# The value products of an attention unit in one run instead of two

## Chip, core and metric

One core of a Trainium2 chip runs the whole kernel. The metric is the device time of one execution in microseconds. Below, PE is TensorE, DVE VectorE, ACT ScalarE, POOL GpSimd and SP SyncE, whose queue issues the DMAs.

## What is computed

Attention over 8 batches and 8 heads with 512 local and 32 global positions of 64 numbers, followed by a gated feed-forward layer over all 4,352 tokens. Local queries see the keys within 32 positions and the 32 global keys; global queries see all 544 keys.

```python
s_ll = np.where(mask, scale * q_l @ k_l.T, -1e9)       # |i - j| <= 32
a_l = sm(np.concatenate([scale * q_l @ k_g.T, s_ll], -1))
out_l = a_l @ np.concatenate([v_g, v_l], 2)
out_g = sm(scale * q_g @ k_all.T) @ v_all
x = concat(out_g, out_l) as (tokens, 512)
xn = x / rms(x) * rms_g
g, val = xn @ w_gate, xn @ w_val                       # 512 -> 1536 each
out = (silu(g) * val) @ w_out                          # 1536 -> 512
```

## The kernel before, in words

The tokens are worked on in nine chunks: eight batches of 512 local tokens and, last, the 256 global ones. While the feed-forward products of one chunk run on TensorE, the attention of a later chunk is done between them. The first two chunks follow an order that is written out by hand (`ORDER`); from chunk 2 on a small planner sets the order, and that is where the change lies.

A chunk's feed-forward work is a list of slots. In chunks 2 to 7 it has 42 slots of 12 fp16 products each (`moe_pair`, its products on line 1108, 7 slots for each of 6 groups) and then 24 slots of 6 products with w_out (`moe_block`, line 1266). After each slot's products the planner's `slot(1, c + 2)` (line 1406) walks through the attention steps that are still to be done and issues each one whose conditions hold, at most one of them with TensorE work. Then the slot's `rest` empties its product bank, on DVE or ACT. The wait for a step is counted in slots: `("A", ..., 1, [("T3", 2), ("V", 4)])` means step A, with TensorE work, at the earliest two slots after T3 and four after V.

The attention of a chunk from the third on consists of two local units (`local_halves`, lines 579 to 748), of four heads each, and one global unit. The steps of a local unit: L and V load queries, keys and values (SP); S makes the scores (line 665); M and N add the mask and find the extreme values on DVE (613), E and F take the exponentials on ACT (627), D divides (DVE 641, POOL 642), T transposes in blocks of 32 on DVE (647, into the tiles `et`); A and B multiply the transposed exponentials with the values (line 708); X and Y copy the result out of four PSUM banks, half by ACT (720) and half by DVE (721), square it (723) and sum the squares on POOL (725). There are twelve local units under the planner.

The values come in eleven key blocks. `blocks` (line 692) sets their order: block 10, the global keys, first, since it covers all queries and starts the sums; each further block adds to the queries that can see it. For each block there are four query/head parts and two heads, eight products on tiles of 32 rows by 64 columns of the array, in fp32. Each of these appears in the profile as two weight loads and two products, so that a unit has 88 products in the program and 176 PE rows and 176 PEld rows in the profile. Of these A has the first five blocks (80 rows) and B the other six (96 rows): `SPLIT, BGAP = 5, 2` (line 93). B comes two slots after A, X one slot after B, Y two after X. The next unit's V waits for B (`"^B"`) in the planner, since it loads into the same tiles.

Of the kernel before, what the change touches and what calls it, by code (L numbers as in the profile page):

```python
# [20 lines left out]
B, H, SL, SG, D = 8, 8, 512, 32, 64  # L21
# [46 lines left out]
def attention_moe_kernel(  # L68
# [21 lines left out]
    EARLY = 2  # L90
    SECOND = 64
    LG = (4, 8)
    SPLIT, BGAP = 5, 2
    GG = (6, 5, 4, 3)
    NORM = {1: (20, 19, 17, 16)}
    NORMS = (22, 21, 19, 17)
# [136 lines left out]
    def attn_bank(name):  # L233
        return psum.tile([P, 512], F32, tag="pa", bufs=4, name=name)
# [192 lines left out]
    def x_part(c, hp):  # L427

        ch = chunks[c]
        if hp % 2 == 0:  # L430
            ch["xx", hp // 2] = pool.tile([P, 2, 512], F32, tag="x", bufs=2, name=f"x{c}_{hp}")
        return ch["xx", hp // 2][:, hp % 2, :]
# [146 lines left out]
    def local_halves(c, b, hp, xt):  # L579
        u = b * (H // 4) + hp  # L580
        w = u - EARLY * (H // 4)
        st = {}
# [93 lines left out]
        def queries(et, m):  # L676

            if m == 10:
                x = et.rearrange("p (b x) -> p b x", b=2)[:, :, 64:448]
                return 0, 8, x.rearrange("p b (t x) -> p b t x", x=96)[:, :, :, QT : 2 * QT]  # L680
            lo, hi = max(0, m - 2), min(7, m)
            n = hi - lo + 1
            a, g = divmod(lo, 4)
            j = m - 4 * a
            o = a * 544 + g * P + (j + (j >= 3) - g) * QT
            if n == 1:
                return lo, n, et[:, o : o + QT]
            off = 0 if o + n * 96 <= 1088 else 64
            x = et[:, o - off : o - off + n * 96].rearrange("p (t x) -> p t x", x=96)
            return lo, n, x[:, :, off : off + QT]  # L690

        blocks = (10, 2, 3, 4, 5, 6, 7, 1, 8, 0, 9)

        def values(ms):
            if ms[0] == blocks[0]:
                st["a"] = [attn_bank(f"a{u}{p}") for p in range(4)]
            ps = st["a"]
            for m in ms:
                for p in range(4):
                    r = slice(p * QT, (p + 1) * QT)  # L700
                    for x in range(2):
                        lo, n, e = queries(st["et"][x][r], m)
                        o = ps[p][x * D : (x + 1) * D, lo * QT : (lo + n) * QT]
                        if n == 8:
                            o = o.rearrange("p (b t q) -> p b t q", b=2, q=QT)
                        elif n > 1:
                            o = o.rearrange("p (t q) -> p t q", q=QT)
                        nc.tensor.matmul(  # L708
                            o,
                            st["v"][x][r, m * D : (m + 1) * D],  # L710
                            e,
                            start=(m == blocks[0]),
                            stop=(m == blocks[-1]),
                            skip_group_check=True,
                        )

        def take(z):
            x = x_part(c, 2 * hp + z)
            xt.append(x)
            nc.scalar.copy(x[:, :256], st["a"][2 * z][:, :256])  # L720
            nc.vector.tensor_copy(x[:, 256:], st["a"][2 * z + 1][:, :256])
            sq = pool.tile([P, 512], F32, tag="w", bufs=3, name=f"sq{u}{z}")
            nc.scalar.activation(sq, x, AF.Square)
            if len(xt) > 1:
                nc.gpsimd.tensor_tensor(sq, sq, chunks[c]["sq"], ALU.add)
            chunks[c]["sq"] = sq

        steps = [
            ("L", load, 0, [("^S", 0)]),
            ("V", load_v, 0, [("^B", 0)]),  # L730
            ("S", scores, 1, [("L", LG[1]), ("^Y", 1)]),
        ]
        wide = 2 if c == EARLY else 3
        for j, (x, bk) in enumerate(((0, 0), (1, 0), (0, 1), (1, 1))):
# [6 lines left out]
                (f"T{j}", lambda x=x, bk=bk: turn(x, bk), 0, [(f"D{j}", 2)]),  # L741
            ]
        return steps + [
            ("A", lambda: values(blocks[:SPLIT]), 1, [("T3", 2), ("V", 4)]),
            ("B", lambda: values(blocks[SPLIT:]), 1, [("A", BGAP)]),
            ("X", lambda: take(0), 0, [("B", 1)]),
            ("Y", lambda: take(1), 0, [("X", 2)]),
        ]

# [612 lines left out]
    for c in range(NCH):  # L1362
        units = [(c, hp, "local") for hp in range(H // 4)] if EARLY <= c < B else []
        for i, g in enumerate(gplan[c]):
            units.insert(i + 1, (g,))
        for i, un in enumerate(units):
            if len(un) == 3:
                xi, steps = 2 * un[1], local_halves(c, c, un[1], chunks[c]["x"])
            else:
                xi, steps = -1, global_unit(*un)  # L1370
            kind = len(un)
            named = {}
            for name, fn, pe, after in steps:
                st = {"name": name, "fn": fn, "pe": pe, "c": c, "x": xi, "after": [], "at": None}
                st["from"] = (FIRST if c == EARLY else UNIT[len(units)])[i]
                for dep, gap in after:
                    if dep[0] == "^":
                        d = seen.get((kind, dep[1:]), [None])[-1]
                    else:
                        d = named[dep]  # L1380
                    if d is not None:
                        st["after"].append((d, gap))
                named[name] = st
                todo.append(st)
                chunks[c]["left"] += 1
            for name, st in named.items():
                seen.setdefault((kind, name), []).append(st)
# [249 lines left out]
```

## Time and profile before

| | |
|---|---|
| median of 3 runs | 935.0 us |
| lowest and highest run | 931.99 and 935.5 us |
| span of the profiled execution, first to last instruction | 930.2 us |
| mean granted TensorE clock | 0.989 |

The time of the profiled execution itself, with what lies around its span, is not listed; the span is 1.8 us under the lowest run and 4.8 under the median. In a profile row, "x" is the number of instructions, and what stands in brackets is the idle time just before, with the engine and operation that ended it; "issue" there means that nothing in the profile explains the idle time. A row of the waits gives the total, the number of times and the longest. A row of the windows gives, for a stretch of time, each engine's busy time and its number of instructions. PE rows are products, PEld rows are weight loads. The chain is the chain of waits that ended last.

### The profile page before, as it was taken

To read this page: it belongs to the slowest core of one execution; us is meant where nothing else is said; L and a number is where in the kernel's file an instruction comes from. 1 tells how busy PE (TensorE), PEld (TensorE's weight loads), DVE (VectorE), ACT (ScalarE), POOL (GpSimd) and SP (SyncE) were. 2 spreads that over 40 slices of the span, in tenths; PEclk is the share of its full clock that TensorE was granted. 3 is DMA by queue.
4 is the path that set the end of the run, shared out by engine and by line. 5 is a ranking of instruction groups with operands and counts; after the bars stand their busy time and mean duration, and the time that the engine had idled before them with its cause. 6 is when DMAs were issued, how large, how long until landed. Compare 5 with 4: busy or idle time off the path is not lost.

```text
span 930.2 us, 26398 instructions
## 1 busy us (share of the span) xinstructions
PE 893.9 (96%) x11028; PEld 612.2 (66%) x11028; DVE 634.0 (68%) x1603; ACT 495.4 (53%) x1232; POOL 253.8 (27%) x219
## 2 busy tenths in 40 slices
PE   5489999999999999999999999999999999999998
PEld 4444455545447885688648874788568865886584
DVE  6999987887884588557775679357846774664331
ACT  6999994555443564456344655356445732543131
POOL 0000000142423262334332353236233432332020
PEclk9699999999999999999999999999999999999999
DMA  9972533686449854495609771685349632787000
GB/s 352 407 288 96 159 120 115 209 265 198 144 119 320 282 180 147 133 299 169 213 24 279 242 238 43 200 279 184 139 136 297 190 95 79 248 273 238 35 1 23
DMA packets 83495, 173.40 MB, mean 186 GB/s; under 512 B 6705, under 2 KB 25393, under 8 KB 83377
## 3 DMA queue, kind: packets, MB, share of 16 engines
q1 hardware_dynamic: 82944, 171.40, 56.1%
q8 instruction: 86, 1.41, 0.6%
q10 hardware_dynamic: 432, 0.33, 0.1%
q14 instruction: 33, 0.26, 0.1%
HBM read 150.21 MB, written 21.50 MB: 185 GB/s over the span
## 4 chain that ended last, share of the span: by engine, by line
PE 82%; DVE 8%; DMA 4%; ACT 3%; issue 1%; POOL 1%; ACTq 0%; DVEq 0%; POOLq 0%
PE pq L1108 36%; PE po L1266 23%; PE p L1205 9%; PE a L708 4%; PE po L1333 3%; PE s L665 3%; DMA k<-in_qk_dram 2%; DMA v<-in_vw_dram 1%; DMA wr<-in_w_in_dram 1%; PE ga L838 1%; PE gs L781 1%; PE gt L824 1%; DVE wf L373 1%; ACT wr L272 1%; DVE t L1302 1%
## 5 line engine op out<-in xcount | busy, mean ns | idle before, releaser
L1108 PEld LDWEIGHTS <-wt 128*128 128x128 f16 x3024 | 292.6, 98 | 40.9 <-issue 5.3
L1266 PE MATMUL po<-wo,h 128*128 128x512 f16 x1080 | 236.2, 379 | 0.0
L1108 PE MATMUL pq<-xh,wt 128*128 128x256 f16 x1152 | 204.3, 273 | 0.0
L1266 PEld LDWEIGHTS <-h 128*128 128x128 f16 x1080 | 105.2, 98 | 123.9 <-issue 1.0
L1108 PE MATMUL pq<-xl,wt 128*128 128x256 f16 x576 | 157.0, 273 | 0.0
L1108 PE MATMUL pq<-ht,wt 128*128 128x256 f16 x1296 | 155.6, 273 | 0.9 <-issue 0.9
L642 POOL TENSOR_TENSOR e<-e,sm 128x512 f32<-128x512 f32 x48 | 50.0, 1042 | 291.4 <-DVE sm L641 287.6
L158 POOL TENSOR_TENSOR h<-t,h 128x512 f16<-128x512 f32 (+1 forms) x90 | 102.4, 1145 | 95.1 <-ACT h L1248 54.2
L1205 PE MATMUL p<-xh,wf 128*128 128x512 f16 x384 | 119.4, 382 | 6.9 <-DVE t L1302 6.3
L1205 PEld LDWEIGHTS <-wf 128*128 128x128 f16 x576 | 55.9, 99 | 74.4 <-issue 12.4
L1140 POOL TENSOR_TENSOR s<-s,s 128x512 f32<-128x512 f32 x36 | 48.2, 1339 | 190.6 <-ACT s L1137 117.9
L627 ACT ACTIVATE e<-e,sm 128x128 f32<-128x128 f32 x192 | 75.2, 393 | 36.6 <-DVE sm L613 36.5
L1170 ACT CAST h<-t 128x512 f16<-128x512 f32 x72 | 44.4, 616 | 57.3 <-DVE t L1162 56.7
L1205 PE MATMUL p<-xl,wf 128*128 128x512 f16 x192 | 73.5, 383 | 0.0
L1162 DVE SCALAR_TENSOR_TENSOR t<-t,c_h,v 128x512 f32<-128x512 f32 x72 | 70.7, 989 | 0.0
L1151 ACT ACTIVATE t<-u,half_inv 128x512 f32<-128x512 f32 x72 | 48.1, 715 | 38.7 <-DVE u L1126 28.6
L1126 DVE TENSOR_TENSOR v<-pq,s 128x512 f32<-128x512 f32 x72 | 49.6, 689 | 24.5 <-PE pq L1108 23.8
L1139 DVE TENSOR_TENSOR s<-pq,s 128x512 f32<-128x512 f32 x36 | 24.9, 691 | 44.3 <-PE pq L1108 42.2
L1133 ACT COPY s<-pq 128x512 f32<-128x512 f32 x36 | 21.0, 584 | 51.3 <-PE pq L1108 51.3
L613 DVE CUSTOM_DVE_ANT_0 e<-s,maskb 128x128 f32<-128x128 f32 x192 | 45.8, 278 | 2.8 <-PE s L665 2.8
L1126 DVE TENSOR_TENSOR u<-pq,s 128x512 f32<-128x512 f32 x36 | 24.9, 691 | 32.9 <-PE pq L1108 24.5
L1158 DVE SCALAR_TENSOR_TENSOR t<-t,u 128x512 f32<-128x512 f32 x72 | 46.9, 679 | 0.5 <-ACT t L1151 0.5
(352 smaller groups left out, 1281.5 us busy)
## 6 DMA issues: line engine op xcount, KB each, us to landing
wt<-wd SPq DMA_DIRECT2D x120, 512.0 KB, 4.8
wr<-in_w_in_dram SPq DMA_DIRECT2D x24, 512.0 KB, 9.9
k<-in_qkb_dram SPq DMA_DIRECT2D x24, 448.0 KB, 6.6
gkq<-in_gkq_dram SPq DMA_DIRECT2D x16, 576.0 KB, 6.5
wt<-wd SPq DMA_DIRECT2D x36, 256.0 KB, 4.7
out_dram<-o SPq DMA_DIRECT2D x34, 256.0 KB, 2.1
v<-in_vb_dram SPq DMA_DIRECT2D x24, 352.0 KB, 7.1
v<-in_vw_dram SPq DMA_DIRECT2D x16, 512.0 KB, 9.7
```

Source lines behind the costliest of these rows:

```text
L158: nc.gpsimd.tensor_tensor(dst, a, b, ALU.subtract)
L613: nc.vector.tensor_tensor_reduce(out=e[:, g, :], in0=ps[:, g * P : (g + 1) * P], in1=late["mask"][:, m * P : (m + 1) * P], scale=-0.125, s ...
L627: nc.scalar.activation(e[:, g, :], e[:, g, :], AF.Exp, bias=sm[:, 0, j + g : j + g + 1], scale=-1.0, accum_out=sm[:, 1, j + g : j + g + 1],)
L642: nc.gpsimd.tensor_tensor(e, e, r.unsqueeze(2).to_broadcast([P, 4, P]), ALU.mult)
L1108: nc.tensor.matmul(ps[:, j * HT : (j + 1) * HT], w[:, j, i, k * P : (k + 1) * P], x[:, k * HT : (k + 1) * HT], start=first, stop=(p in end ...
L1126: nc.vector.tensor_tensor(o, ps, x.rearrange("p (j n) -> p j n", j=2), ALU.add)
L1140: nc.gpsimd.tensor_tensor(s(6), s(6), s(1), ALU.add)
L1151: nc.scalar.activation(t, st["u"][:, j, :], AF.Tanh, scale=half_inv[:, f : f + 1])
L1158: nc.vector.scalar_tensor_tensor(t, t, 1.0, u, ALU.add, ALU.mult)
L1162: nc.vector.scalar_tensor_tensor(t, t, c_h[:, f : f + 1], st["v"][:, j, :], ALU.mult, ALU.mult)
L1205: nc.tensor.matmul(ps[:, :n], rows[:, a, o : o + P], ch[z][k][:, :n], start=(k == 0 and i == 0), stop=(k == NK - 1 and i == 2),)
L1266: nc.tensor.matmul(ps[0], ch["h", f][:, a, j * P : (j + 1) * P], wo[f][:, z, :], start=(f == 0 and q == 0), stop=(f == NF - 1 and q == 2),)
```

## The change

From the third chunk on, the unit's values are one step, A, over all eleven blocks. B is gone, with `SPLIT` and `BGAP`. X now comes one slot after A, and the next unit's V waits for A.

```diff
-    SPLIT, BGAP = 5, 2
...
-        def values(ms):
-            if ms[0] == blocks[0]:
-                st["a"] = [attn_bank(f"a{u}{p}") for p in range(4)]
-            ps = st["a"]
-            for m in ms:
+        def values():
+            ps = st["a"] = [attn_bank(f"a{u}{p}") for p in range(4)]
+            for m in blocks:
...
-            ("V", load_v, 0, [("^B", 0)]),
+            ("V", load_v, 0, [("^A", 0)]),
...
-            ("A", lambda: values(blocks[:SPLIT]), 1, [("T3", 2), ("V", 4)]),
-            ("B", lambda: values(blocks[SPLIT:]), 1, [("A", BGAP)]),
-            ("X", lambda: take(0), 0, [("B", 1)]),
+            ("A", values, 1, [("T3", 2), ("V", 4)]),
+            ("X", lambda: take(0), 0, [("A", 1)]),
             ("Y", lambda: take(1), 0, [("X", 2)]),
```

On TensorE, this is the place in the fourth unit (343.88 us in the profile) where A's first five blocks end. `a` are the four result banks, `et` the transposed exponentials, `v` the values, `pq` a product bank of the feed-forward layer, `wt` its weights. Before:

```order
L708 MATMUL a_4643<-et_4288,v_4020 64x96
L708 MATMUL a_4643<-et_4289,v_4022 64x96
L1108 LDWEIGHTS wt_51_4384
L1108 MATMUL pq_5_4591<-ht_3553,wt_51_4384 128x256
...
L1108 MATMUL pq_5_4608<-xh_3570,wt_52_4422 128x256
L708 MATMUL a_4640<-et_4288,v_4020 64x96
L708 MATMUL a_4640<-et_4289,v_4022 64x96
```

The same place with the change (line 705 is line 708 of before, 1104 is 1108):

```order
L705 MATMUL a_4643<-et_4288,v_4020 64x96
L705 MATMUL a_4643<-et_4289,v_4022 64x96
L705 MATMUL a_4640<-et_4288,v_4020 64x96
L705 MATMUL a_4640<-et_4289,v_4022 64x96
...
L705 MATMUL a_4643<-et_4289,v_4022 64x32
L1104 LDWEIGHTS wt_51_4384
L1104 MATMUL pq_5_4591<-ht_3553,wt_51_4384 128x256
```

The two slots of 12 feed-forward products that stood between the two parts now stand behind the second. Nothing else moves on TensorE: the scores and the global unit's steps keep their places.

On DVE, this is the place behind the fifth unit's run (385.35 us), where a chunk begins. `x` is the attention result, copied from the banks `a`; the additions with `s`, `v` and `u` empty product banks. Before:

```order
L1279 TENSOR_SCALAR o_5215<-po_5127,kk 128x512
L721 COPY x_0_5311<-a_5172 128x256
L1139 TENSOR_TENSOR s_0_5294<-pq_0_5298,s_0_5294 128x512
L1126 TENSOR_TENSOR v_5336<-pq_0_5218,s_0_5294 128x2x256
L721 COPY x_0_5311<-a_5174 128x256
L1126 TENSOR_TENSOR u_5357<-pq_0_5298,s_0_5231 128x2x256
```

With the change (718 is 721 of before, 1275 is 1279, 1135 is 1139, 1122 is 1126):

```order
L1275 TENSOR_SCALAR o_5263<-po_5127,kk 128x512
L718 COPY x_0_5279<-a_5172 128x256
L718 COPY x_0_5279<-a_5174 128x256
L1135 TENSOR_TENSOR s_0_5299<-pq_0_5303,s_0_5299 128x512
L1122 TENSOR_TENSOR v_5341<-pq_0_5266,s_0_5299 128x2x256
L1122 TENSOR_TENSOR u_5357<-pq_0_5303,s_0_5284 128x2x256
```

Both copies now stand ahead of the additions. ACT's copies and squares and POOL's sums (lines 720, 723 and 725) move by the same two slots; the order of SP's DMAs is the same, word for word.

## Prediction

> **What bounds the kernel now.** I read the page first, then the stretches of the steady chunks, then who makes TensorE (PE) wait, and last the rows around one pair of value runs.
>
> ```profile
> span 930.2 us, 26398 instructions
> PE 893.9 (96%) x11028; PEld 612.2 (66%) x11028; DVE 634.0 (68%) x1603; ACT 495.4 (53%) x1232; POOL 253.8 (27%) x219
> q8 instruction: 86, 1.41, 0.6%
> 445.00:545.00 100.00, 100.00 (x1382) 74.23 (x1380) 67.08 (x172) 51.19 (x141) 37.31 (x32) 1.00 0.59 189
> ```
>
> In a steady chunk of 100 us TensorE is never idle, and the next engine, DVE, works for two thirds of it. So a microsecond added to or taken from TensorE's stream there reaches the end, and work moved on DVE, ACT, POOL or SP does not unless it makes TensorE wait. After 190 us it waits for this, and no more:
>
> ```profile
> PE a L708 <- DVE et L647: 2.5, 2, 2.1
> PE pq L1108 <- issue: 0.9, 1, 0.9
> PE a L708 <- issue: 0.2, 1, 0.2
> ```
>
> The first row is the wait of two value runs for the last transposed exponentials (at 242 and 284 us). The other two are waits for nothing that the profile names, and they turn out to price this change.
>
> **The change on TensorE: the seam.** Here is one pair of runs, at 343.88 and 348.08 us, with the products around it.
>
> ```profile
> 343.57 0.27 PE L1108 MATMUL pq<-xl,wt 128*128 128x256 f16 x1
> 343.68 0.27 PE L1108 MATMUL pq<-xh,wt 128*128 128x256 f16 x1
> 343.88 1.54 PE L708 MATMUL a<-et,v 32*64 32x256 f32 x80
> 345.35 1.48 PE L1108 MATMUL pq<-ht,wt 128*128 128x256 f16 x12
> ...
> 347.87 0.27 PE L1108 MATMUL pq<-xh,wt 128*128 128x256 f16 x1
> 348.08 1.31 PE L708 MATMUL a<-et,v 32*64 32x96 f32 x96
> 349.32 0.28 PE L1108 MATMUL pq<-xh,wt 128*128 128x256 f16 x1
> ```
>
> Products start 0.11 us apart; going into a value run costs 0.20 and coming out again some 0.15 after the last value product's start. The second run costs TensorE 349.32 - 347.87 - 0.11 = 1.34 us. Its 96 products themselves, from the first start to the last, take 1.31 less the last one's own 0.22, so 1.09. Joined to the first run it pays no entry and no exit of its own: at most 1.34 - 1.09 = 0.25 us saved. [...] Nothing is computed less: the 176 products of a unit stay.
>
> **The change on the other engines.** The copies of step X (ACT 0.37 us, DVE 0.42), its square and POOL's sum come two slots earlier, Y's too, and SP may load the next values two slots earlier.
>
> ```profile
>   DVE x L721: 33.4, 11
>   ACT x L720: 8.8, 11
> SPq L602 <- PE a L708: 9.2, 3, 8.3
> ```
>
> These are waits of other engines for the value products: DVE stands 33.4 us in all at the head of its queue for them. Behind DVE's copy stand the additions that empty the product banks (L1139, L1126), but those need products that TensorE makes only after the run, so a copy of 0.42 us ahead of them is hidden in the next slot of 1.3 us. If that cover went, it would cost 24 times 0.42, 10 us; with a third of DVE idle I cost it at nothing. SP's order stays word for word. Its loads only come free sooner, and TensorE waits for no load after 190 us. The two waits for the transposes stay as they are: the run starts in its old slot, and the transposes are not moved.
>
> **The change on instruction supply.** This is the term that decides. The queue q8 brings 86 packets for 22,056 TensorE instructions (11,028 products and as many weight loads): 256 each. Where TensorE stopped for no named reason:
>
> ```profile
> 421.58 0.83 PE L1108 MATMUL pq<-ht,wt 128*128 128x256 f16 x6
> 423.33 0.83 PE L1108 MATMUL pq<-ht,wt 128*128 128x256 f16 x6 [0.92 <-issue]
> ...
> 289.06 0.80 PE L708 MATMUL a<-et,v 32*64 32x96 f32 x45
> 290.07 0.77 PE L708 MATMUL a<-et,v 32*64 32x64 f32 x51 [0.21 <-issue]
> ...
> 390.55 0.03 issue
> 390.57 0.45 PE a L708 x27
> ```
>
> The stops end at 423.33, 290.07 and 390.57. I counted the instructions between these ends:
>
> ```profile
> 290.06:423.32 133.26, 132.31 (x1916) 102.17 (x1915) 86.58 (x215) 66.56 (x169) 46.99 (x39) 1.00 0.66 215
> 390.56:423.32 32.76, 31.83 (x511) 27.46 (x511) 19.53 (x43) 15.13 (x29) 9.46 (x8) 1.00 0.88 289
> ```
>
> 3,831 lie between the first two, nine short of 15 times 256, and 1,022 between the last two, two short of 4 times 256; the few missing are waits that stand in TensorE's queue as instructions of their own. So all three stops fall exactly on the border between two packets. The packet before each, found by narrowing the window of the DMA view until it just held one, ran from 420.70 to 421.82, from 287.70 to 288.62 and from 388.11 to 389.07, in this order:
>
> ```profile
> q8 instruction: 1, 0.02, 6.0%
> ...
> q8 instruction: 1, 0.02, 6.0%
> ...
> q8 instruction: 1, 0.02, 6.0%
> ```
>
> TensorE went on 1.51, 1.45 and 1.50 us after the packet's end. I read this as starvation: a packet's instructions can be used 1.5 us after it lands, and it is asked for about when TensorE enters the page before. A stretch that burns 256 instructions faster than that makes TensorE wait. Products burn 24 in 1.31 us, 14 us a page. A value run burns 160 in the 1.30 us between the first and last start of its first part, and 192 in the 1.09 of its second: under 2 us a page. Neither part alone holds a page; joined they hold 352.
>
> [...]
>
> Where the page borders lie in each unit follows by counting from the border at 290.07 to the unit's first product:
>
> ```profile
> 290.06:343.87 53.81, 53.80 (x734) 47.24 (x733) 35.44 (x91) 32.09 (x83) 21.47 (x19) 1.00 0.78 250
> 290.06:385.35 95.28, 95.28 (x1232) 70.28 (x1231) 66.30 (x171) 50.25 (x138) 37.28 (x31) 1.00 0.58 191
> 290.06:445.15 155.09, 154.13 (x2115) 121.58 (x2114) 102.50 (x263) 83.51 (x223) 58.99 (x50) 1.00 0.64 209
> 283.53:290.06 6.53, 5.92 (x151) 4.42 (x150) 1.34 (x2) 1.17 (x2) 0.78 (x2) 1.00 0.99 318
> ```
>
> At 343.88: 1,467, so the next border (1,536) is 69 instructions into the unit, 67 with the waits counted. At 385.35: 2,463 against 2,560, about 91 with six waits. At 445.16: 4,229 against 4,352, about 113 with ten. At 283.9, counted backwards: 301 less 256, about 44. From 343.88 to 445.16 the border moves 46 later, and it does so with each further chunk: 138, 160, 185, 207, 232, 254 in the later units. Only where the first border falls before about 130 does the second one, 256 on, fall in the joined run of 352 or just behind it. Those are four units: 283.9, 343.9, 385.35 and 445.16. Two more packets, from 345.55 to 346.74 and from 447.45 to 448.76, serve the second and the fourth:
>
> ```profile
> q8 instruction: 1, 0.02, 6.1%
> ...
> q8 instruction: 1, 0.02, 6.1%
> ```
>
> The unit at 343.88, step by step: it passes the first border at 344.5, as before. The second, at instruction 323, it would reach at 345.2 + 163 x 5.7 ns = 346.1. The packet can be used at 346.74 + 1.5 = 348.2: a stop of 2.1 us. Then 29 instructions (0.2 us), the exit (0.15) and the two slots of products that used to stand between the runs (24 at 0.109, 2.6 us): the next product starts at 351.2 against 349.32 before, **+1.9 us**. Before, those two slots covered the wait; now they come after it.
>
> The other three take their ends from the chain:
>
> ```profile
> 290.84 0.22 PE pq L1108
> ...
> 391.02 0.22 PE pq L1108
> ...
> 450.66 0.21 PE pq L1108
> ```
>
> At 283.9: usable at 290.1 in both; before, 100 instructions were left and the slots done (290.8), now 52 are left and then 2.6 us of products, 293.2: **+2.4**. At 385.35: usable at 390.57; 391.0 before, 393.4 now: **+2.4**. At 445.16: the border lies 17 instructions behind the run, reached at 448.7, usable at 448.76 + 1.5 = 450.26; then 31 instructions of products, 1.7 us, and the pipeline: 452.1 against 450.66, **+1.4**.
>
> **The sum.** Stops 2.4 + 1.9 + 2.4 + 1.4 = +8.1; the seam in the eight other units 8 x -0.2 = -1.6. Together +6.5 us, 0.7%, on the profiled span of 930.2. The runs' median of 935.0 lies 4.8 above that span, the lowest, 931.99, only 1.8; I add the shift to the median: **941.5**.
>
> Bounds: from the first border to use it took 5.0, 3.7, 4.4 and 4.2 us in the four units. If every packet were as quick as 3.7, +4.5 would be left. If slow, a unit loses at most its two slots, about 2.5, and a fifth unit (486.6, border 42 instructions behind the run) up to 0.9: +8.5. With the runs' own scatter of 3.5 us, from 938 to 944.5 for this case.
>
> **Rivals.** *The fetch is hidden*: the stops were of another kind, or the packet is asked for sooner when the run burns faster. For it: the stops of before add up to under 2 us in 700. Then the seam alone counts: 932.6, not slower. It decides where packets can be used within 1.8 us of the first border; the quickest here took 3.7. [...] Chance 0.16. *The earlier copies and loads shorten DVE's busy stretch* from 192 to 245 us, so that the wait of 2.1 us for the transposes goes as well and fetch stays hidden: 935.0 - 2.4 - 2.5 = 930.1. Against it: only two copies pass the fold's sums there, and DVE's work is the same. Chance 0.05. *More units starve*: the value loads now start under the packet of a run and hold it up, so that the units at 545, 587 and 746 us stop too, at 1.5 us each: 946. Against it: their second border lies 60 or more instructions behind the run, or the packet lands before the run begins. Chance 0.07. The forecast keeps 0.72.
>
> **Chances.** Half a per cent, 4.7 us, is about what a measurement of this kernel can tell from no change. Of the forecast's 0.72, 0.56 lies above 939.7 and 0.16 below; with the third rival slower has 0.62. The first rival and the rest of the forecast make the same, 0.32; faster has 0.06, the second rival and the first one's scatter. The range 933 to 944.5 holds nearly all of the forecast and about half of the first rival.
>
> **What would show it.** Right: in the four units the joined run reads as two groups with an idle of 2 to 3 us on TensorE put down to issue, ending 1.5 us after a q8 packet, and the joined runs of the other units read as one group of some 2.4 us (the two first ones aside, where the transposes may be waited for). Wrong: all twelve runs of one piece and a span near 928; or idle put down to et, to a load, or to a bank that a copy holds.

## The result, and the profile after

| | before | after |
|---|---|---|
| median of 6 runs | 934.7 us | 944.17 us |
| lowest and highest | 931.99 and 936.04 us | 941.98 and 948.48 us |
| the profiled run | 931.99 us, span 930.2, clock 0.989 | 948.48 us, span 946.7, clock 0.978 |

The change makes the kernel 1.0% slower: ratio 1.0102, 95% interval 1.0084 to 1.0121, or 9.5 us between the medians. The profiled run of before is the quickest of its six and that of after the slowest of its six, so the two traces lie 16.5 us apart, more than the kernels do; the rows below explain the 16.5, and a later section says what of it is left in the medians.

First the page of after: the span, the busy times, the packets of q8, and the shares of the chain.

```profile
span 946.7 us, 26404 instructions
PE 900.2 (95%) x11028; PEld 618.2 (65%) x11028; DVE 624.1 (66%) x1603; ACT 495.3 (52%) x1232; POOL 252.7 (27%) x219
q8 instruction: 86, 1.41, 0.6%
PE 82%; DVE 9%; DMA 4%; ACT 3%; issue 2%; POOL 0%; ACTq 0%; DVEq 0%
```

TensorE has the same 11,028 products and is still the bound, but two things have grown: its busy time, by 6.3 us for the same work, and "issue" in the chain. The waits of TensorE after 190 us give the second its size:

```profile
PE a L705 <- issue: 7.1, 3, 2.9
PE pq L1104 <- issue: 4.1, 3, 1.9
PE a L705 <- DVE et L646: 2.5, 2, 2.1
```

The wait for the transposes is what it was. The unnamed waits went from 1.1 us to 11.2. Here they are on TensorE's timeline, in the third to the sixth unit; the number in brackets is the idle time ahead of the row:

```profile
286.76 1.25 PE L705 MATMUL a<-et,v 32*64 32x96 f32 x88
290.93 0.66 PE L705 MATMUL a<-et,v 32*64 32x32 f32 x27 [2.91 <-issue]
...
350.00 2.38 PE L705 MATMUL a<-et,v 32*64 32x256 f32 x160
354.52 0.35 PE L705 MATMUL a<-et,v 32*64 32x32 f32 x16 [2.15 <-issue]
...
395.12 2.55 PE L705 MATMUL a<-et,v 32*64 32x256 f32 x172
399.74 0.42 PE L705 MATMUL a<-et,v 32*64 32x32 f32 x4 [2.07 <-issue]
...
461.70 1.05 PE L1104 MATMUL pq<-ht,wt 128*128 128x256 f16 x8
464.64 1.04 PE L1104 MATMUL pq<-ht,wt 128*128 128x256 f16 x4 [1.90 <-issue]
...
503.98 2.58 PE L705 MATMUL a<-et,v 32*64 32x256 f32 x176
```

Three value runs are broken near their ends (16 products of 176 are left in the second, 4 in the third); the fourth run is whole and the stop lies eight products behind it. The last row is a unit with nothing missing, one group of 2.58 us. The packet of q8 ahead of each stop, found by narrowing the DMA view:

```profile
q8 instruction: 1, 0.02, 3.0%
...
q8 instruction: 1, 0.02, 3.4%
...
q8 instruction: 1, 0.02, 5.1%
...
q8 instruction: 1, 0.02, 4.9%
```

They ended at 289.70, 353.12, 398.30 and 463.36; TensorE went on 1.23, 1.40, 1.44 and 1.28 us later. Two more stops of the kind stand outside the value runs: 1.80 us at 437.26 behind the products of a step S, which was 0.92 us at 423.33 in before, and 0.44 us at 543.40.

Now the busy time. These are rows of after's chain: what stands behind the four stops, and the same stretches behind two units without one.

```profile
285.75 2.26 PE a L705 x103
288.01 2.91 issue
291.59 14.65 PE pq L1104 x108
350.07 2.31 PE a L705 x117
352.38 2.15 issue
354.87 7.01 PE pq L1104 x48
...
400.16 13.30 PE pq L1104 x108
...
464.64 6.10 PE pq L1104 x40
...
504.05 2.51 PE a L705 x129
506.56 11.90 PE pq L1104 x108
562.89 2.51 PE a L705 x133
565.40 5.35 PE pq L1104 x48
```

The same 108 products took 11.90 us in one place and 14.65 and 13.30 behind a stop; 48 took 5.35 and 7.01; and 40, which at that pace would take 4.41, took 6.10. They were slower because the granted clock was halved there, 0.50 against 1.00. The windows show where (us, TensorE's busy time and its instructions, the granted clock, DMA share, GB/s):

```profile
351.81:355.22 3.41, 1.26 (x76) 1.00 0.66 206
355.22:358.63 3.41, 3.41 (x18) 0.50 0.93 293
396.18:399.59 3.41, 1.49 (x131) 1.00 0.82 217
433.72:437.13 3.41, 1.74 (x82) 1.00 0.51 163
437.13:440.55 3.42, 3.29 (x31) 1.00 0.51 160
```

Behind the stop at 354.52 the clock is 0.50 for one stretch of 3.41 us. The stop at 437.26 leaves the clock alone. In all there are five such drops after 190 us, from 246.0 (behind the wait for the transposes), 290.37, 355.22, 399.59 and 464.45; the one from 290.37 lasts 6.83 us, the others 3.41. Before had none between 190 us and the end.

### The profile page after: what moved, and what is told of

It is laid out like the page before. It is cut to its first block, busy times and chain, and to the rows that moved or that the text cites. A ratio compares the mean times of both kernels' runs of the same rounds, so it can differ in the third digit from the quotient of the medians.

```text
span 946.7 us, 26404 instructions
## 1 busy us (share of the span) xinstructions
PE 900.2 (95%) x11028; PEld 618.2 (65%) x11028; DVE 624.1 (66%) x1603; ACT 495.3 (52%) x1232; POOL 252.7 (27%) x219
## 3 DMA queue, kind: packets, MB, share of 16 engines
q8 instruction: 86, 1.41, 0.6%
## 4 chain that ended last, share of the span: by engine, by line
PE 82%; DVE 9%; DMA 4%; ACT 3%; issue 2%; POOL 0%; ACTq 0%; DVEq 0%
PE pq L1104 36%; PE po L1262 22%; PE p L1201 9%; PE a L705 3%; PE po L1329 3%; PE s L664 3%; DMA k<-in_qk_dram 2%; DMA v<-in_vw_dram 1%; DMA wr<-in_w_in_dram 1%; PE ga L834 1%; PE gs L777 1%; PE gt L820 1%; ACT wr L271 1%; DVE t L1301 1%; DVE t L1298 1%
## 5 line engine op out<-in xcount | busy, mean ns | idle before, releaser
L1104 PEld LDWEIGHTS <-wt 128*128 128x128 f16 x3024 | 297.2, 99 | 47.1 <-issue 8.4
L1104 PE MATMUL pq<-xh,wt 128*128 128x256 f16 x1152 | 206.4, 276 | 0.4 <-issue 0.4
L1104 PE MATMUL pq<-ht,wt 128*128 128x256 f16 x1296 | 159.6, 277 | 3.7 <-issue 3.7
L1158 DVE SCALAR_TENSOR_TENSOR t<-t,c_h,v 128x512 f32<-128x512 f32 x72 | 61.1, 855 | 0.0
L722 POOL TENSOR_TENSOR sq<-sq,sq 128x512 f32<-128x512 f32 x18 | 23.0, 1276 | 92.1 <-ACT sq L720 76.0
```

The costliest lines, as they stand in the source:

```text
L1104: nc.tensor.matmul(ps[:, j * HT : (j + 1) * HT], w[:, j, i, k * P : (k + 1) * P], x[:, k * HT : (k + 1) * HT], start=first, stop=(p in end ...
L1158: nc.vector.scalar_tensor_tensor(t, t, c_h[:, f : f + 1], st["v"][:, j, :], ALU.mult, ALU.mult)
```

## The experiments

All ratios are to the kernel before on the same chip.

**The joined run alone.** X and V are put back to their old places, so that DVE, ACT, POOL and SP do everything in before's order.

```diff
-            ("V", load_v, 0, [("^A", 0)]),
+            ("V", load_v, 0, [("^A", 2)]),
...
-            ("X", lambda: take(0), 0, [("A", 1)]),
+            ("X", lambda: take(0), 0, [("A", 3)]),
```

> The values in one run, but X, Y and the next unit's value load two slots later, so that DVE, ACT, POOL and SP have the very order of before: only TensorE's stream is changed. Starvation (TensorE comes to a page border before the packet can be used): as slow as the change, 941 to 946 us, with the same four stops in the third to sixth unit. Moved steps (the earlier copies and loads do the harm): back at 932 to 935 us, with no stops in the runs.

945.16 us, ratio 1.0114 (1.0089 to 1.0139): all of the loss is still there. So are the waits:

```profile
PE a L705 <- issue: 7.3, 3, 3.7
PE pq L1104 <- issue: 3.2, 3, 1.9
```

The four stops end at 292.26, 354.80, 399.15 and 460.43, in the same units. Two smaller ones are in the second row: 0.58 us at 505.31, in the products behind the seventh unit's run, and 0.73 at 540.43. The earlier copies and loads neither cost nor brought anything that shows.

**The borders moved by half a packet.** The changed kernel with 64 tiny products more in an early group, 128 instructions for TensorE, so that every later border falls 128 instructions elsewhere. If the borders decide, other units stop. The control is the kernel before with the same products.

```diff
-            for j, f in enumerate(fs):
+            for j, f in enumerate(fs * 9 if g == 1 else fs):
+                j = j % len(fs)
```

> The change, with 64 tiny products repeated early on TensorE (128 instructions more; they give the same sums again), so that every later page border falls 128 instructions earlier in each unit. Starvation: the third and fourth unit (borders now at 172 and 194) and the fifth run through without a stop, and the stops of 1 to 2.5 us move to the first two units (32, 77) and the seventh to eleventh (10, 32, 57, 79, 104), seven or more in all: 950 to 960 us. Any cause that belongs to the units themselves (their transposes, loads, banks): the stops stay in the third to sixth unit and the time within 2 us of the change, 944 to 946.

953.65 us, ratio 1.0203 (1.0173 to 1.0233). The timeline around the first unit, the fourth and the eighth:

```profile
202.28 0.73 PE L706 MATMUL a<-et,v 32*64 32x64 f32 x33 [5.51 <-issue]
...
356.07 2.58 PE L706 MATMUL a<-et,v 32*64 32x256 f32 x176
...
559.38 0.69 PE L706 MATMUL a<-et,v 32*64 32x64 f32 x33 [2.23 <-issue]
```

The runs of the third to the sixth unit are whole now. The first, second and eighth to eleventh stop instead (from one product's start to the next across the stop 5.73, 0.91, 2.45, 1.22, 2.02 and 2.18 us), and the twelfth for 0.93. The shift tells which units stop, as the borders said, with one miss: the seventh, which was among the seven expected, ran through, and the twelfth, which was not, stopped.

> The kernel before with the same 64 early products, as a control for them. Starvation: the split runs cannot starve much wherever the borders fall, so 933 to 938 us. If the early products themselves cost time, it shows here: over 938.

The control took 939.62 us, ratio 1.0058 (1.0036 to 1.0079), more than expected: the extra products start the first value run at 195.1 instead of 192.3 us, and two small stops come with the shift, 1.53 us idle ahead of 202.32 and 0.94 ahead of 229.42. Against its own control the joined run therefore costs 14.0 us with these borders, 9.5 with the old ones.

**One slot between the runs instead of two.**

```diff
-    SPLIT, BGAP = 5, 2
+    SPLIT, BGAP = 5, 1
```

> The kernel before with one slot of products between the two runs instead of two. Starvation: half the cover, so that the third to sixth unit stop for 1.7, 0.6, 1.1 and 0.9 us and lose about 1.2, 0.7, 1.2 and 1.1, 4 us in all and perhaps 1 to 3 more where the clock drops behind a stop: 937 to 942, between the two kernels. Seam alone: as before, 933 to 936. A dense run of one piece as the cause: as before.

938.99 us, ratio 1.0043 (1.0027 to 1.0059): 3.9 us more than before, between the two kernels. The waits:

```profile
PE a L708 <- issue: 3.0, 3, 1.7
PE pq L1108 <- issue: 1.7, 1, 1.7
```

The first row is three of the four units, which stop for 1.68, 0.85 and 0.52 us; the sixth, for which 0.9 us was expected, does not. The second row is none of them but the stop behind step S, now at 431.09. With half the products between the runs, 3.0 us of waiting come out from behind them, a third of the 9.0 that the four units have in the change.

**One run only where the border allows it.** Units 1 and 8 to 12 are joined, the others split as before.

```diff
+    ONE, LATE = (0, 7, 8, 9, 10, 11), {}
...
+        split = len(blocks) if w in ONE else SPLIT
...
-            ("A", lambda: values(blocks[:SPLIT]), 1, [("T3", 2), ("V", 4)]),
-            ("B", lambda: values(blocks[SPLIT:]), 1, [("A", BGAP)]),
+            ("A", lambda: values(blocks[:split]), 1, [("T3", 2 + LATE.get(w, 0)), ("V", 4)]),
+            ("B", lambda: values(blocks[split:]), int(w not in ONE), [("A", 0 if w in ONE else BGAP)]),
```

> One run in six units alone (the first and the eighth to twelfth), where no second page border falls in the run; two runs in the other six. Starvation with a seam of 0.29 us a unit: no stop in these six, 1.7 us less than before, 933 to 934. A dense run of one piece as harmful in itself: half of the change's loss, 939 to 940.

932.35 us, ratio 0.9973 (0.996 to 0.9987), 2.4 us quicker; none of the six joined runs stops. The same joining that loses 9.5 us in all twelve units gains in these six.

**And the run moved where it does not.** In the third, fourth and fifth unit the joined run comes 3, 3 and 5 slots later, so that its first border falls before the run; the second and the sixth stay split. The rest of the edit is as in the run before.

```diff
+    ONE, LATE = (0, 2, 3, 4, 6, 7, 8, 9, 10, 11), {2: 3, 3: 3, 4: 5}
```

> One run in ten units, two runs in the second and sixth. In the third, fourth and fifth the run comes 3, 3 and 5 slots later, so that 72 to 120 instructions of products go first and the borders fall at -27, -5 and -28 and at 229, 251 and 228 instead of at 44, 67 and 91 and at 300, 323 and 347. Starvation: the packet is asked for before the run begins, no stop over 0.5 us in any of the three, no drop of the clock behind them, and ten seams of 0.29 saved: 931 to 934. Any cause that belongs to these units or to a run of one piece: the stops of 2 to 3 us stay, 941 or more.

929.1 us, ratio 0.9942 (0.9919 to 0.9964): quicker than both kernels, and than the 931 to 934 that were expected. The third, fourth and fifth unit on its timeline:

```profile
289.88 2.58 PE L713 MATMUL a<-et,v 32*64 32x256 f32 x176
...
348.12 2.58 PE L713 MATMUL a<-et,v 32*64 32x256 f32 x176
...
391.90 1.93 PE L713 MATMUL a<-et,v 32*64 32x256 f32 x113
394.41 0.87 PE L713 MATMUL a<-et,v 32*64 32x64 f32 x63 [0.57 <-issue]
```

Two are whole; the third stops for 0.57 us, a little over the 0.5 that was allowed for. Of the 5.6 us, ten seams at 0.29 (below) are 2.9, and a wait of 0.4 us for the transposes in the third unit goes, since its run now comes later; what the rest is was not separated.

**The changed kernel again**, unedited, on the same chip as the last two.

> The change once more, beside the two others. Starvation: the same four stops at the same instructions, 943 to 946, whatever their length in this execution. A chance event as the cause: stops elsewhere.

943.18 us, ratio 1.0083 (1.0057 to 1.011), with the same four stops. But only two of them were followed by half clock (0.50 from 292.86 and from 354.30; 1.00 behind the other two), though they are about as long as in the first trace. That left open what decides it.

**What decides the clock.** The drops of the first trace begin 64.85, 44.37 and 64.86 us apart (290.37, 355.22, 399.59, 464.45): 19, 13 and 19 times 3.413. In each of the nine traces so far every change of the clock lies on one such grid, with another offset in each run. So I laid the grid over the traces and compared each window's busy time with the clock of the next, and put what came out to the test in two more runs.

> The changed kernel a third time, unedited, for one question: after which of its stops does the granted clock of TensorE halve? Theory: the clock is decided on a grid of windows of 3.413 us that runs on its own, from the start of the run to its end (in the nine traces so far all changes of the clock in one run lie on one such grid, at another offset in each run). A window after 190 us in which products are in TensorE for less than 0.48 of the time is followed by half clock, one with more than 0.53 is not, and full clock comes back behind a window that is busy for more than 0.85. So a stop of 2.0 to 2.4 us drops the clock when a border of the grid cuts it by less than about 0.4 to 0.7 us, and does not when the border cuts it near its middle: of the four stops 2 to 4 drop it. Rival 1, the length of the stop alone: stops over 2.2 us drop it, shorter ones do not. Rival 2, a whole idle window is needed: no stop under 3.4 us drops it. Time 942 to 946 us by all.

> The changed kernel with 64 tiny products more at the start (128 instructions of TensorE), a second time. Same question as for the run beside it, with other stops: 5.5, 0.9, 2.2, 1.2, 2.0, 2.0 and 0.9 us at the 1st, 2nd, 8th to 12th unit. Theory of the grid: half clock behind each window of the grid that is busy for less than 0.48, none behind one over 0.53; the long stop fills a window whole wherever the grid lies, so it drops the clock in every run; the stops of 0.9 and 1.2 us can leave no window under 0.53 and never drop it. Rival 1, length alone: those over 2.2 us. Rival 2, a whole idle window: only the long one. Time 951 to 956 us.

In the first of these (941.38 us, one run, beside 933.85 for before; a little under what was expected), the windows around the third, fourth, fifth and sixth unit:

```profile
284.90:288.31 3.41, 1.50 (x124) 1.00 1.00 328
288.31:291.72 3.41, 0.87 (x29) 0.50 0.98 358
...
349.75:353.16 3.41, 2.14 (x155) 1.00 0.57 174
353.16:356.57 3.41, 3.41 (x34) 1.00 0.99 335
394.13:397.54 3.41, 1.56 (x17) 1.00 0.88 257
397.54:400.95 3.41, 3.41 (x19) 0.50 0.99 325
455.57:458.98 3.41, 2.23 (x117) 1.00 0.70 240
```

A window that is busy for 1.50 or 1.56 us of 3.41 (0.44 and 0.46) is followed by half clock; with 2.14 or 2.23 it is not. The stop of 1.89 us in the fifth unit, which fell almost whole into one window, dropped the clock, and a stop of 2.21 us in the second run (948.59 us, one run; 951 to 956 were expected), behind which the clock stayed at 1.00, did not. There only the 4.94 us stop of the first unit did, behind a window busy for 0.96 us. That refutes length alone, and a whole idle window is not needed. Over all eleven traces, from 190 us to the end of the work, every drop follows a window that was busy for at most 0.51 of its length, and no window under 0.48 went without one; from 0.49 to 0.51 both happened. Full clock came back only behind a window busy for 0.94 or more; the long drops are those whose next window was not (0.84 in the first trace of the change).

## Why the prediction was right, and where it was off

The predicted 941.5 us was 2.7 below the measured median, inside the range, and the sign and the mechanism held. That the median is inside is in part luck: the range's top of 944.5 was worked out without the clock, the median lies 0.3 us under it, and three of the six runs lie above that top. By the prediction's steps:

**The four stops: right.** They were named ahead by unit, and they came in these four and in no other value run. From the start of a run to the first product behind it, by the chain, without the two slots of 2.73 us that stood between the parts before: third unit 5.84 against 5.96 - 2.73, +2.6; fourth 4.80 against 5.44 - 2.73, +2.1; fifth 4.97 against 5.60 - 2.73, +2.1; sixth 5.39, less eight products of 0.11, against 5.43 - 2.73, +1.8. Together +8.6 where the sum had +8.1 (2.4, 1.9, 2.4 and 1.4). That the border and not the place of the copies decides was shown by moving each apart: the joined run alone lost the same, and 128 instructions more at the start moved the stops to other units.

**Stops on packet borders: right, beyond the three that it rested on.** In all eleven traces together TensorE has 57 unnamed idles of over 0.15 us behind 190 us. Counted in its instructions, with the waits in its queue, every one of them ends a multiple of 256 from every other one of its trace, and the remainder, counted from the start, is the same in all eleven, the shifted kernels included.

**A packet usable 1.5 us after it lands: near.** Across the four stops it was 1.23 to 1.44, over the 57 from 1.08 to 1.53.

**Asked for about when TensorE enters the page before: too simple.** It held for the four stops, where the packet began 0.8 to 2.7 us after that border. But in the shifted kernel the packet of the seventh unit began at 494.16 us, 2.5 us before its first border, and that of the first unit 5.0 us behind it.

**The seam: under-sized.** The bound of 0.25 us a unit was too low. A split unit of before, by its chain:

```profile
486.69 1.47 PE a L708 x66
488.16 2.73 PE pq L1108 x24
490.89 1.24 PE a L708 x71
```

5.44 us, of which 24 products at after's 11.90 / 108 us would be 2.64; the whole run in after takes 2.51. That is 5.44 - 2.64 - 2.51 = 0.29 us. The working took entry and exit off the second part only; the joined run's own products are closer too: 2.58 - 0.22 = 2.36 us from first to last start against 1.54 + 1.31 - 2 x 0.22 = 2.41 in two parts. Eight units make -2.3, not -1.6. The 0.2 us a unit that the sum takes, 2.4 for all twelve in the rivals, is shown by no run; the traces show 0.29.

**Copies and loads at no cost: right,** by the joined run alone.

**What was missing: the clock.** The sum priced a stop by its idle time alone. In these traces a stop that left a window of 3.41 us on the grid less than about half busy (under 0.48 always, over 0.51 never) was also followed by half clock, 0.50, in TensorE's next 3.41 us. In the profiled run: 14.65 - 11.90, 13.30 - 11.90, 7.01 - 5.35, and 6.10 - 4.41, together +7.5; the drop behind the wait for the transposes at 246 adds about 1.4 by the chain. With stops +8.6, seams -2.3, the longer stop at 437 +0.9 and one of 0.4 at 543, that is 16.5, the difference of the two spans.

In the medians the clock counts for less, because the offset of the grid differs from run to run (a border at 290.37 us in the first trace of the change, at 292.86 and 288.31 in its two later ones) and with it the number of drops; the mean clock was 0.978 to 0.984 in the six runs of after. Time below full speed, one less the mean clock times the span, is on average 12.0 us in the 39 runs of before in the first two sets of experiments and 17.2 in ten of after, a difference of 5.3 before rounding; for the profiled pair it is 10.6, of which the rows found 8.9. By the same share the medians hold some 4.4 us of clock. With 8.6 - 2.3 us of stops and seams that is 10.7 (an estimate), against 9.5 measured. So the step that was mis-sized is the sum's price of a stop, by the clock it costs; the errors in the stops (+0.5) and in the seams (-0.7) nearly cancel.

**Slips in the working that change little.** With 3.7 us for every packet the lower bound is 8.1 - 1.3 - 0.7 - 0.5 - 1.6 = +4.0, not +4.5. The first part of a split run burns a page in 2.1 us (256 / 160 x 1.30), not under 2.

**The rivals.** A hidden fetch is refuted by 11.2 us of unnamed waits that end on packet borders and move with them. The transposes' wait did not go (2.5 us in both). More units starving from earlier loads did not happen: with the loads back in their old place the same four units stopped, and there the seventh as well, for 0.58 us, which the prediction's bounds had allowed for.

**Left open.** What delays a packet. From the first border until the next packet could be used it took 3.8 to 4.9 us in the four units. Two units of the shifted kernel are the ends of it: the first, which waited 5.5 us, and the seventh, which ran through a border that was expected to stop it. These are the stretches in which their packets were due (us, TensorE's busy time and its instructions, the granted clock, DMA share, GB/s):

```profile
195.00:200.00 5.00, 1.77 (x132) 1.00 0.99 300
494.00:497.00 3.00, 3.00 (x29) 1.00 0.02 5
```

The first unit's packet began at 199.79, at the end of 5 us with the DMA engines 99% busy. The seventh's, with hardly any other traffic, had landed at 495.04, before the run began at 496.65, so there was nothing to wait for. That fits the other DMA traffic as the cause, but no run changed the traffic alone, so it is not shown; nor is it known when exactly a packet is asked for.

## What to carry to other kernels

When the bounding engine waits for "issue", count the instructions between the ends of such waits. If the count is a multiple of the packet's size (256 here), find where the next borders fall before packing many small instructions together. Larger products between two bursts of tiny ones can be what hides the fetch (here 24 products, 2.73 us), and moving the burst by a few slots can be worth more than removing the seam: 929.1 us against 943.18 on the same chip, for the same products. And price each stop of TensorE with the clock that it may cost: in the first trace of the change the stops of 1.90 to 2.15 us in the value runs or just behind one cost another 1.4 to 1.7 us, and the one of 2.91 us, where the drop lasted two windows, 2.75.

## What the runs showed of the hardware

- In before and in the change, q8 brought 86 packets, 1.41 MB, for TensorE's 22,056 products and weight loads. The 57 unnamed stops over 0.15 us after 190 us, in eleven traces, ended, within each trace, multiples of 256 TensorE instructions apart, 1.08 to 1.53 us after a packet had landed; 128 instructions more at the start moved the stops to other units.
- In each of the eleven traces the granted clock changed only on one grid of 3.413 us, at another offset in each run. After 190 us, half clock (0.50) followed every window with products in TensorE for under 0.48 of it and none with over 0.51; full clock (1.00) came back only behind a window that was busy for 0.94 or more (0.84 was not enough). The same stop was therefore followed by half clock in one run and not in the next.
- Splitting a run of small fp32 products on tiles of 32 by 64 cost 0.29 us in a stream of fp16 products, entry and exit included.
